# A two-branch mix kernel: first stage on ssm_k in float32 on two row tiles, and the convolution's fill given out in small weighted steps

## The chip, the core and the metric

The kernel runs on one core of a Trainium2 chip. The metric is the device time of one execution in microseconds; the time before the change is the median of three runs, 1002.43 us (1001.9 to 1003.99). The profile comes from one more execution of the same program, which took 1001.61 us.

TensorE (PE in the profile) multiplies matrices into PSUM; VectorE (DVE), ScalarE (ACT) and GpSimd (POOL) work on tiles in SBUF; SyncE (SP), ACT and POOL issue transfers.

## The reference

Two branches on the same 2048 tokens of 512 numbers are mixed by a gate of each token. Branch A is a short causal convolution over 4 taps, a product with `v`, a causal convolution as long as the sequence (computed by FFT) and a product with `q`. Branch B is a mixture of 8 experts, of which each token takes 2.

```python
x = A_q
g = sigmoid((x * gate_w).sum(-1, keepdims=True))

# branch A
k_shift = sum(k_pad[:, t:t+S, :] * shift_k[:, ks-1-t] for t in range(4))
kv = k_shift * v
y = irfft(rfft(pad(kv)) * rfft(pad(ssm_k)))[:S] + kv * ssm_D
a = q * y

# branch B
logits = x @ w_router                    # 8 experts, best 2, softmax over the 2
hg = silu(x @ w_gate[e]);  hu = x @ w_up[e]
b = sum(gate[e] * ((hg * hu) @ w_down[e]) for the 2 experts e)

return g * a + (1 - g) * b
```

## The kernel before

**The main line is the experts.** After routing, the tokens of each expert are gathered in tiles of 128 rows and turned (`gather`, `load_rows`, `turn_rows`, L359 to L395). Each of 8 experts has 11 "up tiles" of up to 128 hidden columns (`FT`), so 88 in all. One up tile (`up`, L752) loads one weight tile `raw`, splits it into a high part (ACT, `gh`) and a rest (DVE, `gl`), and runs, for each of two halves of the expert's tokens and for gate and up, 4 x 3 matmuls: 48 in all. Every product of two float32 matrices is made of three matmuls of float32r parts (`mm3`, L186). After each half ACT takes Silu of the gate's PSUM tile, DVE multiplies by the up's PSUM tile (L784), ACT and DVE split the result (`hh`, `hl`) for the down product. Down products (`down`) and the turning back and scattering of an expert's rows (`finish`, L846) are put into a list `tasks`, of which two are done after each up tile.

**Routing** comes first (L428 to L637) and is written out by hand: inside `tc.manual_schedule` the order of the instructions on every engine is the order of the program (`ordered = True`). It leads from the logits over a ranking on DVE to `list0` (L625), a product that tells which tokens the first expert gets; `read(0)` turns it into indices `gidx` (L597) and POOL gathers the first rows (L366). The rest of the routing (`routing`, L643; `values`, `places` and `read`, L569 to L605) runs beside the first expert's up tiles. Its tiles `hots` and `vals` lie in the second buffers of the tags `xl` and `xh`, so the second expert's rows can only be turned when the last list has been made.

**The convolution is the fill.** It is an FFT in two stages over 16 planes `pl` of 128 rows and 32 frequencies `k1`:

- stage 1 on `ssm_k`, one plane at a time: load `kr`, product with a fixed matrix, two results `t` = 0 and 1 of 128 rows, ACT empties the PSUM tile (L229) and writes it to `kd` in HBM (L230, on ACT's queue)
- stage 1 on `k * v` (`x_stage1`, L271): the four taps on DVE (eight operations of 128x512), a split, the same product, to `xd`
- stage 2 (`x_stage2`, L290): `kd` and `xd` back, products with a matrix of each `k1` (loaded by POOL), the complex product, the way back, to `zd`
- the last stage (`y_stage`, L324): two products that sit side by side on the columns of the array (the second is issued right after the first, L331), times gate and `q`, added to the output.

The product of stage 1 has 64 rows to sum over, for each of `t` = 0 and 1. With `pairs` (L197) the high part of such a half is put on 64 partitions and the rest on the other 64, and two float32r matmuls over 128 partitions do one `t` (L224); with an unsplit tile one float32 matmul over 64 partitions does it (L227), which the trace shows as two records. Six planes (1 to 6) are done inside the hand-written part, at the points `plan(0)` to `plan(4)`, by the string `SEQ` (L57): `o` is a plane's product, `l` a load, `s4` a split of the fifth plane with both subtractions on POOL. The other ten are part of the fill, with one subtraction on POOL and one on DVE (L260).

The fill outside the hand-written part is a list of generators: `k_stage1`, `x_stage1`, `x_stage2`, `y_stage`, with empty entries between (`BUB`). A `tick` (L343) takes one more from the list and moves every live one to its next `yield`. Two ticks are made before the first up tile (L639); then, after each up tile, so many that the count of ticks follows the count of up tiles (L903), to be through at 0.97 of the 88. Outside the hand-written part the program's order is only a priority: a planner with a simulated clock (`schedule_with_timeline_sim`) places the instructions. `after(...)` keeps some of them behind a given instruction of their engine.

PSUM: tag `m` (`misc`) has two buffers for the convolution, tag `y` (`turned`) three, for turned rows, lists and down products, tag `gu` three.

Of the kernel before, what the change touches and what calls it, by code (L numbers as in the profile page):

```python
# [15 lines left out]
ALU = mybir.AluOpType  # L16
# [113 lines left out]
def gated_mix(ctx: ExitStack, tc: tile.TileContext, a, out):  # L130
# [45 lines left out]
    def t2k(tag, bufs, name, dt=F32):  # L176
        return fp.tile([P, D], dt, tag=tag, bufs=bufs, name=name)
# [15 lines left out]
    def rows(t, pl):  # L193
        return t[pl * P:(pl + 1) * P, :]


    def pairs(x, name, eng):  # L197
        ts = []
        for t in range(2):
            own, other = slice(64 * t, 64 * t + 64), slice(64 - 64 * t, 128 - 64 * t)  # L200
            hl = t2k(("fh", "fl")[t], (FH, FL)[t], f"{name}{t}", F32R)
            with after("act k"):
                act.activation(hl[own], x[own], AF.Copy)
            with after("dve k"):
                eng[t].tensor_sub(hl[other], x[own], hl[own].bitcast(F32))
            ts.append(hl)
        return ts

    def load(tag, bufs, name, src, late=False):
# [6 lines left out]
                sync.dma_start(r, src)  # L216
        return r

    def stage1(hl, dst, pl, name):
        for t in range(2):  # L220
            p = misc(f"{name}p{t}")
            if isinstance(hl, list):
                for i in range(2):
                    pe.matmul(p, cr[:, i, :P], hl[t], start=(i == 0), stop=(i == 1))  # L224
            else:
                half = slice(64 * t, 64 * t + 64)
                pe.matmul(p, c1[half], hl[half], start=True, stop=True)  # L227
            ev = t2k("ev", 4, f"{name}e{t}")
            act.activation(ev, p, AF.Copy)  # L229
            act.dma_start(dst[:, :, t::2, pl, :], ev)  # L230

    def mats(src, k1, tag):
        m = fp.tile([P, 2, P], F32R, tag=tag, bufs=3, name=f"{tag}{k1}")
# [1 line left out]
            pool.dma_start(m, src[k1])  # L235
        return m

    kr, ks = {}, {}
# [24 lines left out]

    krows = {}

# [2 lines left out]
            krows[r] = load("A", 6, f"krow{r + 3}", rows(a["kpad"], r + 3))  # L268
        return krows[r]

    def x_stage1(pl):  # L271
        if pl == 0:
            with after("sp"):
                sync.dma_start(sk, a["sk"].unsqueeze(0).to_broadcast([P, TAPS, D]))
        for r in range(-3, 1):
            krow(pl + r)
        v = load("T", 3, f"v{pl}", rows(a["v"], pl))
        yield
        acc = t2k("B", BB, f"acc{pl}")
        tmp = t2k("T", 3, f"tmp{pl}")  # L280
        dve.tensor_mul(acc, krow(pl), sk[:, 0])
        for tap in range(1, TAPS):
            dve.tensor_mul(tmp, krow(pl - tap), sk[:, tap])
            dve.tensor_add(acc, acc, tmp)
        dve.tensor_mul(acc, acc, v)
        hl = pairs(acc, f"xs{pl}", (dve, dve))
        yield
        stage1(hl, xd, pl, f"xs{pl}")

    def x_stage2(k1):  # L290
        flat = lambda t: t[k1].rearrange("c f a d -> (c f a) d")
        rk = load("B", BB, f"kl{k1}", flat(kd))
        rx = load("B", BB, f"xl{k1}", flat(xd))
        mf = mats(a["c_mf"], k1, "mf")
        mi = mats(a["c_mi"], k1, "mi")
        yield
        hk = halves(rk, f"k2{k1}")
        hx = halves(rx, f"x2{k1}")
        yield
        pk = misc(f"k2p{k1}")  # L300
        mm3(pk, mf[:, 0], mf[:, 1], *hk)
        krr = t2k("A", 6, f"krr{k1}")
        kii = t2k("A", 6, f"kii{k1}")
        for t, s0 in ((krr, 0), (kii, 64)):
            for h in range(2):
                act.activation(t[64 * h:64 * h + 64, :], pk[s0:s0 + 64, :], AF.Copy)
        p = misc(f"x2p{k1}")
        mm3(p, mf[:, 0], mf[:, 1], *hx)
        sw = t2k("T", 3, f"sw{k1}")
        act.activation(sw[0:64, :], p[64:128, :], AF.Copy, scale=-1.0)  # L310
        act.activation(sw[64:128, :], p[0:64, :], AF.Copy)
        y = krr
        dve.tensor_mul(y, p, krr)
        dve.tensor_mul(sw, sw, kii)
        dve.tensor_add(y, y, sw)
        hl = halves(y, f"y2{k1}")
        yield
        pz = misc(f"zp{k1}")
        mm3(pz, mi[:, 0], mi[:, 1], *hl)
        ev = t2k("ev", 4, f"ze{k1}")  # L320
        act.activation(ev, pz, AF.Copy)
        act.dma_start(flat(zd), ev)

    def y_stage(pl):  # L324
        r = [load("B", BB, f"zl{pl}_{t}", zd[:, :, t::2, pl, :]) for t in range(2)]
        xr = load("A", 6, f"xr{pl}", rows(a["q"], pl))
        yield

        p = misc(f"yp{pl}")
        last = pe.matmul(p[64:], c2, r[1], start=True, stop=True).ins  # L330
        with tc.issue_after(last):  # L331
            pe.matmul(p[:64], c2, r[0], start=True, stop=True)
        ev = t2k("ev", 4, f"ye{pl}")
        dve.scalar_tensor_tensor(ev, p, G[:, pl:pl + 1], xr, op0=ALU.mult, op1=ALU.mult)
        pool.dma_start(rows(out[:S, :], pl), ev, accum_op=ALU.add)

    wait = lambda n: [iter(()) for _ in range(n)]
    fill = ([k_stage1(i) for i in k_order[SEQ_N:]] + wait(BUB[0]) + [x_stage1(i) for i in range(PL)] + wait(BUB[1]) +
            [x_stage2(i) for i in range(NK)] + wait(BUB[2]) + [y_stage(i) for i in range(PL)])
    fill.reverse()  # L340
    live = []

    def tick():  # L343
        if fill:
            live.append(fill.pop())
        for g in list(live):
            if next(g, live) is live:
                live.remove(g)

    anchor = {}  # L350

# [43 lines left out]
            turn_rows(r, n, g[n], xh, xl)  # L395

    xs = {}

    def ticks(n):
        for _ in range(n):  # L400
            tick()


    CM = max(CAPS)
# [51 lines left out]
    def plan(k):  # L456
        for w in SEQ[k].split():
            i = int(w[1:])
            if w[0] == "l":
                k_load(k_order[i])  # L460
            elif w[0] == "s":
                k_split(k_order[i], (pool, pool))
            else:
                k_out(k_order[i])

# [170 lines left out]
    ordered = False  # L636
    for _ in rows0:  # L637
        pass
    ticks(2)  # L639

    early.close()

# [95 lines left out]
    def expert(r):  # L738
# [13 lines left out]
        def up(ft):  # L752
# [20 lines left out]
            for h, (n0, nn) in enumerate(parts):  # L773
                sl = slice(n0, n0 + nn)
                pp = []
                for u, tag in ((0, "g"), (1, "u")):
                    p = ps.tile([P, 512], F32, tag="gu", bufs=3, name=f"{tag}{r}_{ft}_{h}")
                    for kt in range(KT):
                        mm3(p[:fw, :nn], ghv[:, u, kt], glv[:, u, kt], xh[:, kt, sl], xl[:, kt, sl],
                            start=(kt == 0), stop=(kt == KT - 1))  # L780
                    pp.append(p)
                sg = mp.tile([P, HM], F32, tag="sg", bufs=3, name=f"sg{r}_{ft}_{h}")
                act.activation(sg[:fw, :nn], pp[0][:fw, :nn], AF.Silu)  # L783
                dve.tensor_mul(sg[:fw, :nn], sg[:fw, :nn], pp[1][:fw, :nn])  # L784
# [78 lines left out]

        return begin, up, down, finish

    total, done, seen = len(fill) + len(live), 0, 0
    n_up = E * len(FT) * SPREAD
    tasks = []
    ahead = None
    rest = routing()  # L870
    order_c = [*range(2, len(chunks)), 1]
    for r in range(E):
# [3 lines left out]
        for ft in range(len(FT)):  # L876
# [6 lines left out]
            if r + 1 < E:  # L883
# [15 lines left out]
            seen += 1  # L899
            if r == 0 and ft >= Z0:  # L900
                for i in range(Z1 * (ft - Z0), min(Z1 * (ft - Z0 + 1), ROWS // P)):
                    clear(i)
            while done < min(total, int(total * seen / n_up)):  # L903
                tick()
                done += 1
        if r not in TM:
            tasks += [(finish, n) for n in range(tiles(r))]
    while fill or live:
        tick()
    while tasks:  # L910
        f, *x = tasks.pop(0)
        f(*x)
# [87 lines left out]
```

## Time and profile before

| what | value |
|---|---|
| median of 3 runs | 1002.43 us (1001.9 to 1003.99) |
| profiled execution | 1001.61 us |
| its span, first to last instruction | 999.8 us |
| mean granted TensorE clock | 0.981 |
| PE, weight load, DVE, ACT, POOL busy | 960.8, 881.6, 685.9, 582.5, 182.2 us |
| moved by DMA | 178.19 MB |

A line of a grouped view names the line of the program, the engine, the operation, the tile written and the tiles read, the shape and the count; then the busy time and, after the bar, the idle time of the engine before it and who ended it. A matmul's record is longer than the distance to the next one, since matmuls are pipelined: the distance from start to start is what it costs. A PE that counts as fully busy can still issue more or fewer matmuls.

### The profile page before, as it was taken

What the parts mean: (1) busy time and instruction counts of PE and PEld (TensorE: products, weight loads), DVE (VectorE), ACT (ScalarE), POOL (GpSimd) and SP (SyncE); (2) the same over time, 40 slices, a digit from 0 to 9 for tenths busy, and PEclk for the clock granted to TensorE, in tenths of its full rate; (3) what the DMA queues carried; (4) which work ended last, traced back from release to release, by engine and by line L of the source; (5) the groups of instructions that cost most, each with busy time, mean ns of one, the idle gap of its engine ahead of it and who ended that gap; (6) DMA issues with size and microseconds to landing.
All of it is one profiled execution on the core that took longest, in us unless ns stands there. A gap on an engine that the chain in (4) does not pass through costs nothing. (4 is left out here: it accounts for less than half of the span.)

```text
span 999.8 us, 18820 instructions
## 1 busy us (share of the span) xinstructions
PE 960.8 (96%) x6944; PEld 881.6 (88%) x6944; DVE 685.9 (69%) x1301; ACT 582.5 (58%) x1102; POOL 182.2 (18%) x177
## 2 busy tenths in 40 slices
PE   7888999999999999999999999999999999999995
PEld 2487999989998999999999999998898999768894
DVE  7699679979998855656677468665776666554541
ACT  5485434455555645678667777676777777234230
POOL 1342102110202112131111411022120300113002
PEclk9599999999999999999999999999999999999998
DMA  8775395566656437575445754466565734799613
GB/s 285 249 250 185 112 357 190 167 160 213 201 171 168 147 115 215 176 166 169 137 142 180 181 180 159 141 187 141 156 195 159 206 117 135 217 327 241 162 31 42
DMA packets 88401, 178.19 MB, mean 178 GB/s; under 512 B 10641, under 2 KB 19601, under 8 KB 88178
## 3 DMA queue, kind: packets, MB, share of 16 engines
q1 hardware_dynamic: 52882, 116.73, 35.6%
q0 software_dynamic: 19296, 30.08, 15.3%
q10 hardware_dynamic: 16128, 30.15, 8.3%
q8 instruction: 56, 0.92, 0.4%
q14 instruction: 39, 0.32, 0.1%
HBM read 133.34 MB, written 43.57 MB: 177 GB/s over the span
## 5 line engine op out<-in xcount | busy, mean ns | idle before, releaser
L187 PE MATMUL g<-xh,gh 128*128 128x256 f32 (+13 forms) x704 | 203.9, 290 | 5.6 <-DVE sg L784 5.6
L187 PE MATMUL u<-xh,gh 128*128 128x256 f32 (+13 forms) x704 | 202.0, 287 | 6.0 <-ACT sg L783 5.1
L189 PE MATMUL g<-xh,gl 128*128 128x256 f32 (+13 forms) x704 | 201.6, 286 | 0.0
L188 PE MATMUL g<-xl,gh 128*128 128x256 f32 (+13 forms) x704 | 201.5, 286 | 0.0
L188 PE MATMUL u<-xl,gh 128*128 128x256 f32 (+13 forms) x704 | 201.2, 286 | 0.0
L189 PE MATMUL u<-xh,gl 128*128 128x256 f32 (+13 forms) x704 | 201.1, 286 | 0.0
L187 PEld LDWEIGHTS g<-xh,gh 128*128 128x128 f32 (+1 forms) x704 | 131.5, 187 | 15.7 <-DVE sg L784 8.8
L187 PEld LDWEIGHTS u<-xh,gh 128*128 128x128 f32 (+1 forms) x704 | 131.2, 186 | 10.8 <-ACT sg L783 6.9
L784 DVE TENSOR_TENSOR sg<-sg,u 128x256 f32<-128x256 f32 (+13 forms) x176 | 74.9, 426 | 90.5 <-PE u L189 56.4
L188 PEld LDWEIGHTS g<-xl,gh 128*128 128x128 f32 (+1 forms) x704 | 131.6, 187 | 3.1
L189 PEld LDWEIGHTS u<-xh,gl 128*128 128x128 f32 (+1 forms) x704 | 131.3, 186 | 3.1 <-issue 1.6
L188 PEld LDWEIGHTS u<-xl,gh 128*128 128x128 f32 (+1 forms) x704 | 131.2, 186 | 2.7 <-issue 0.8
L189 PEld LDWEIGHTS g<-xh,gl 128*128 128x128 f32 (+1 forms) x704 | 131.7, 187 | 1.3
L187 PE MATMUL yp<-hh,dh 128*128 128x266 f32 (+10 forms) x440 | 128.0, 292 | 2.1 <-ACT yr L853 1.9
L188 PE MATMUL yp<-hl,dh 128*128 128x266 f32 (+10 forms) x440 | 127.4, 290 | 0.0
L189 PE MATMUL yp<-hh,dl 128*128 128x266 f32 (+10 forms) x440 | 127.1, 290 | 0.0
L768 DVE TENSOR_TENSOR gl<-raw,gh 128x1024 fp32r<-128x1024 f32 (+1 forms) x88 | 105.2, 1195 | 28.4 <-ACT gh L766 26.3
L783 ACT ACTIVATE sg<-g 128x256 f32<-128x256 f32 (+13 forms) x176 | 67.5, 385 | 87.0 <-PE g L189 83.0
L766 ACT ACTIVATE gh<-raw 128x1024 fp32r<-128x1024 f32 (+1 forms) x88 | 91.3, 1037 | 40.9 <-PE u L188 30.1
L785 ACT ACTIVATE hh<-sg 128x256 fp32r<-128x256 f32 (+13 forms) x176 | 73.6, 419 | 70.1 <-DVE sg L784 68.9
L786 DVE TENSOR_TENSOR hl<-sg,hh 128x256 fp32r<-128x256 f32 (+13 forms) x176 | 75.2, 428 | 36.8 <-ACT hh L785 35.9
L366 POOL DMA_INDIRECT xg<-in_q,gidx x37 | 48.5, 1311 | 227.0 <-PE xgp L375 209.4
(1072 smaller groups left out, 1898.3 us busy)
## 6 DMA issues: line engine op xcount, KB each, us to landing
raw<-in_wgu SPq DMA_DIRECT2D x77, 512.0 KB
rd<-in_wd SPq DMA_DIRECT2D x77, 256.0 KB
kl<-kd SPq DMA_DIRECT2D x32, 256.0 KB
xl<-xd SPq DMA_DIRECT2D x32, 256.0 KB
zd<-ze ACTq DMA_DIRECT2D x32, 256.0 KB
zl<-zd SPq DMA_DIRECT2D x32, 256.0 KB
out<-zt SPq DMA_DIRECT2D x21, 256.0 KB
krow<-in_kpad SPq DMA_DIRECT2D x19, 256.0 KB
```

The source lines that it names most:

```text
L187: pe.matmul(p, wh, hi, start=start, stop=False)
L188: pe.matmul(p, wh, lo, start=False, stop=False)
L189: pe.matmul(p, wl, hi, start=False, stop=stop)
L366: anchor["pool"] = pool.indirect_dma_start(out=xg[:w], out_offset=None, in_=a["q"], in_offset=bass.IndirectOffsetOnAxis(ap=gidx[:w, col:co ...
L766: act.activation(gh[:, :n], raw[:, :n], AF.Copy)
L768: dve.tensor_sub(gl[:, :n], raw[:, :n], gh[:, :n].bitcast(F32))
L783: act.activation(sg[:fw, :nn], pp[0][:fw, :nn], AF.Silu)
L784: dve.tensor_mul(sg[:fw, :nn], sg[:fw, :nn], pp[1][:fw, :nn])
L785: act.activation(hh[:fw, sl], sg[:fw, :nn], AF.Copy)
L786: dve.tensor_sub(hl[:fw, sl], sg[:fw, :nn], hh[:fw, sl].bitcast(F32))
```

## The change

Stage 1 on `ssm_k` no longer splits. Every plane is done in float32 by two matmuls over 64 partitions each, on the upper and the lower half of the array's rows; both PSUM tiles are taken first, `t` = 1 is issued before `t` = 0, and outside the hand-written part `t` = 0 is held right behind it. In the hand-written part even planes take their PSUM tiles from tag `y`. `s4` and its branch are gone, as are `k_split` and the two early ticks.

The generators become lists of steps, each with a place (relative to its item's number), a weight and a function. `woven` sorts the steps of all items of a stage by place, and adds a pause. The steps are given out by weight, as far as the share of up tiles done allows, at four points of each up tile: after each half, at its end, and after the tasks. The taps of `x_stage1`, one step before, are in three steps, its split in a fourth; stage 2 has five steps.

```diff
-BUB = (1, 1, 3)
-SEQ = "|o0 l5 o1|o2 s4 o3||o4 o5".split("|")
+SEQ = "|o0 l5 o1|o2 o3||o4 o5".split("|")
...
+    def out1(p, dst, pl, t, name):
+        ev = t2k("ev", 4, f"{name}e{t}")
+        act.activation(ev, p, AF.Copy)
+        act.dma_start(dst[:, :, t::2, pl, :], ev)
+
     def stage1(hl, dst, pl, name):
         for t in range(2):
             p = misc(f"{name}p{t}")
-            if isinstance(hl, list):
-                for i in range(2):
-                    pe.matmul(p, cr[:, i, :P], hl[t], start=(i == 0), stop=(i == 1))
-            else:
-                half = slice(64 * t, 64 * t + 64)
-                pe.matmul(p, c1[half], hl[half], start=True, stop=True)
-            ev = t2k("ev", 4, f"{name}e{t}")
-            act.activation(ev, p, AF.Copy)
-            act.dma_start(dst[:, :, t::2, pl, :], ev)
+            for i in range(2):
+                pe.matmul(p, cr[:, i, :P], hl[t], start=(i == 0), stop=(i == 1))
+            out1(p, dst, pl, t, name)
+
+    def stage1_f32(x, dst, pl, name):
+        where = turned if ordered and pl % 2 == 0 else misc
+        ps_ = [where(f"{name}p{t}") for t in range(2)]
+        first = None
+        for t in (1, 0):
+            half = slice(64 * t, 64 * t + 64)
+            with tc.issue_after(first) if first is not None and not ordered else nullcontext():
+                first = pe.matmul(ps_[t], c1[half], x[half], start=True, stop=True).ins
+        for t in range(2):
+            out1(ps_[t], dst, pl, t, name)
...
-    def k_split(pl, engines):
-        ks[pl] = pairs(kr[pl], f"ks{pl}", engines)
-
     def k_out(pl):
-        stage1(ks.get(pl, kr[pl]), kd, pl, f"ks{pl}")
-
-    def k_stage1(pl):
-        if pl not in kr:
-            k_load(pl)
-            yield
-        if pl not in ks:
-            k_split(pl, (pool, dve))
-            yield
-        k_out(pl)
+        stage1_f32(kr[pl], kd, pl, f"ks{pl}")
+
+    def k_steps(pl):
+        yield -1.5, .3, lambda: k_load(pl)
+        yield 0, 1.3, lambda: k_out(pl)
...
+    def x1_steps(pl):
...
+        yield -1.2, .3, fetch
+        yield 0, 2.1, lambda: taps(0, 2)
+        yield .25, 1.4, lambda: taps(2, 3)
+        yield .5, 2.1, lambda: taps(3, 4)
+        yield .75, 1.4, split
+        yield 1.3, 1.0, lambda: stage1(t["hl"], xd, pl, f"xs{pl}")
...
+    def x2_steps(k1):
...
+        yield -1.9, .3, fetch
+        yield -.8, 1.4, split
+        yield 0, 1.0, forward_k
+        yield .3, 3.5, forward_x
+        yield 1.2, 1.0, back
...
+    def y_steps(pl):
...
+        yield -1.2, 2.0, fetch
+        yield 0, 2.5, turn
...
+    def woven(items, pause):
+        steps = [(i + at, i, w, do) for i, item in enumerate(items) for at, w, do in item]
+        steps.sort(key=lambda x: x[:2])
+        return [(w, do) for _, _, w, do in steps] + [(pause, lambda: None)]
+
+    fill = (woven([k_steps(i) for i in k_order[SEQ_N:]], 3) + woven([x1_steps(i) for i in range(PL)], 6) +
+            woven([x2_steps(i) for i in range(NK)], 9) + woven([y_steps(i) for i in range(PL)], 0))
+    load_all = sum(w for w, _ in fill)
+    spent = [0.0]
+
+    def fill_to(share):
+        while fill and spent[0] + fill[0][0] / 2 <= share * load_all:
+            w, do = fill.pop(0)
+            spent[0] += w
+            do()
...
-    ticks(2)
...
             for h, (n0, nn) in enumerate(parts):
...
                 dve.tensor_sub(hl[:fw, sl], sg[:fw, :nn], hh[:fw, sl].bitcast(F32))
+                fill_up(.25 + .25 * h)
...
             st[ft] = (hh, hl, dh, dl)
+            fill_up(.75)
...
+    def fill_up(part):
+        fill_to((seen[0] + part) / n_up)
...
-            while done < min(total, int(total * seen / n_up)):
-                tick()
-                done += 1
+            fill_up(0)
...
-    while fill or live:
-        tick()
+    fill_to(2)
```

More of the change, by code (lines that the diff above doesn't have):

```diff
@@ L236, in mats @@
         return m
-    kr, ks = {}, {}
+    kr = {}
     k_order = [*range(1, PL), 0]
@@ L269, in krow @@
         return krows[r]
[L271 to L288, printed above, removed]
@@ L290, in x_stage2 @@
-    def x_stage2(k1):
-        flat = lambda t: t[k1].rearrange("c f a d -> (c f a) d")
[L292 to L348, printed above, removed]
+    def x1_steps(pl):
+        t = {}
+        def fetch():
+            if pl == 0:
+                with after("sp"):
+                    sync.dma_start(sk, a["sk"].unsqueeze(0).to_broadcast([P, TAPS, D]))
+            for r in range(-3, 1):
+                krow(pl + r)
+            t["v"] = load("T", 3, f"v{pl}", rows(a["v"], pl))
+        def taps(first, last):
+            if first == 0:
+                t["acc"] = t2k("B", BB, f"acc{pl}")
+                t["tmp"] = t2k("T", 3, f"tmp{pl}")
+                dve.tensor_mul(t["acc"], krow(pl), sk[:, 0])
+            for tap in range(max(first, 1), last):
+                dve.tensor_mul(t["tmp"], krow(pl - tap), sk[:, tap])
+                dve.tensor_add(t["acc"], t["acc"], t["tmp"])
+            if last == TAPS:
+                dve.tensor_mul(t["acc"], t["acc"], t["v"])
+        def split():
+            t["hl"] = pairs(t["acc"], f"xs{pl}", (dve, dve))
+        yield -1.2, .3, fetch
[4 more added lines that the diff above has]
+        yield 1.3, 1.0, lambda: stage1(t["hl"], xd, pl, f"xs{pl}")
@@ new lines, in y_steps, with fetch, turn @@
+    def y_steps(pl):
+        t = {}
+        def fetch():
+            t["r"] = [load("B", BB, f"zl{pl}_{h}", zd[:, :, h::2, pl, :]) for h in range(2)]
+            t["xr"] = load("A", 6, f"xr{pl}", rows(a["q"], pl))
+        def turn():
+            p = misc(f"yp{pl}")
+            last = pe.matmul(p[64:], c2, t["r"][1], start=True, stop=True).ins
+            with tc.issue_after(last):
+                pe.matmul(p[:64], c2, t["r"][0], start=True, stop=True)
+            ev = t2k("ev", 4, f"ye{pl}")
+            dve.scalar_tensor_tensor(ev, p, G[:, pl:pl + 1], t["xr"], op0=ALU.mult, op1=ALU.mult)
+            pool.dma_start(rows(out[:S, :], pl), ev, accum_op=ALU.add)
+        yield -1.2, 2.0, fetch
+        yield 0, 2.5, turn
@@ L397, in gated_mix @@
     xs = {}
-    def ticks(n):
-        for _ in range(n):
-            tick()
     CM = max(CAPS)
@@ L460, in plan @@
                 k_load(k_order[i])
-            elif w[0] == "s":
-                k_split(k_order[i], (pool, pool))
             else:
@@ L864, in expert @@
         return begin, up, down, finish
-    total, done, seen = len(fill) + len(live), 0, 0
+    seen = [0]
     n_up = E * len(FT) * SPREAD
+    def fill_up(part):
+        fill_to((seen[0] + part) / n_up)
     tasks = []
@@ L898, in gated_mix @@
                     next(ahead, None)
-            seen += 1
+            seen[0] += 1
             if r == 0 and ft >= Z0:
```

36 lines of the change are left out of this document (35 added, 1 removed).

## The prediction

> **What bounds the kernel now.** I read the page first, then the busy times by stage, then who ended PE's waits, then the timeline of the stages where PE is not full.
>
> ```profile
> span 999.8 us, 18820 instructions
> PE 960.8 (96%) x6944; PEld 881.6 (88%) x6944; DVE 685.9 (69%) x1301; ACT 582.5 (58%) x1102; POOL 182.2 (18%) x177
> ```
> ```profile
> 20.00:44.00 24.00, 19.36 (x57) 7.79 (x56) 15.79 (x54) 10.85 (x19) 8.00 (x7) 0.55 0.68 231
> 57.00:95.00 38.00, 32.04 (x219) 29.20 (x217) 37.43 (x76) 24.38 (x46) 10.16 (x7) 1.00 0.66 219
> 95.00:120.00 25.00, 24.20 (x219) 23.17 (x220) 19.44 (x48) 10.56 (x21) 5.97 (x4) 1.00 0.33 109
> 150.00:220.00 70.00, 67.78 (x519) 66.98 (x519) 61.92 (x113) 34.17 (x67) 14.52 (x10) 1.00 0.60 184
> 220.00:300.00 80.00, 80.00 (x602) 78.29 (x601) 77.49 (x140) 43.32 (x83) 9.07 (x5) 1.00 0.56 184
> 300.00:340.00 40.00, 36.28 (x266) 35.11 (x265) 32.43 (x57) 22.11 (x44) 8.91 (x5) 0.96 0.60 165
> 340.00:860.00 520.00, 517.19 (x3792) 492.26 (x3791) 335.86 (x607) 363.79 (x690) 89.47 (x102) 1.00 0.56 163
> ```
>
> The columns of the second view are the stretch, its length, then PE, PEld, DVE, ACT and POOL, granted clock, DMA share, GB/s. PE bounds the kernel: from 340 to 860 us it lacks 2.8 us of 520. So relief of other engines is worth nothing there. What can be gained is PE's missing time elsewhere: 38.00 - 32.04 = 6.0 us in 57 to 95, 0.8 in 95 to 120, 2.2 + 3.7 = 5.9 in 150 to 220 and 300 to 340, and the start, where PE waits for routing. The row of 220 to 300 matters too: DVE at 77.49 of 80 and PE full, so a DVE filled with taps does not by itself stop PE.
>
> ```profile
> PE g L187 <- DVE sg L784: 4.1, 3, 1.4
> PE u L187 <- DVE sg L784: 0.8, 1, 0.8
> ```
> ```profile
> PE u L187 <- ACT sg L783: 4.0, 2, 2.2
> PE yp L187 <- ACT yr L853: 1.9, 1, 1.9
> ```
> ```profile
> ACT yr L853 <- DMA out<-yr,sidx: 25.7, 10, 5.9
> ```
>
> The first two rows are PE's waits in 55 to 95, the next two those in 200 to 350, the last is of the whole run (total, times, longest). Early, PE waits for DVE, which is late with the product that frees a gate or up PSUM tile. Later it waits behind ACT, whose queue stands at L853 until an older scatter has let go of `yr`.
>
> **Why DVE is late early.**
>
> ```profile
> L205 POOL TENSOR_TENSOR ks<-kr,ks x12: 1261/1456/1832, 30.3 to 97.2; 64x512 fp32r<-64x512 f32 x12
> L205 DVE TENSOR_TENSOR ks<-kr,ks x10: 686/687/1665, 57.0 to 100.8; 64x512 fp32r<-64x512 f32 x10
> ```
> ```profile
> 47.72 0.21 DVE L652 TENSOR_TENSOR s<-s 128x64 f32<-128x64 f32 x1
> 47.85 0.22 DVE L654 TENSOR_SCALAR r<-r 128x128 f32<-128x128 f32 x1
> ```
> ```profile
> 54.45 1.31 DVE L656 TENSOR_TENSOR s<-s,rc 128x64 f32<-128x64 f32 x1
> ```
>
> The split of `ssm_k` costs DVE ten subtractions of 0.69 us, and more through POOL: beside a subtraction on POOL an operation that takes DVE 0.21 us (L652) takes 1.31 (L656, same shape). With some eight such collisions after 50 us, at 1.1 us each, the split holds DVE for about 10 x 0.69 + 8 x 1.1 = 16 us of the 44 us to 101, an estimate from these rows.
>
> **The change part by part.**
>
> *The start.* The fifth plane's split on POOL sits on routing's path:
>
> ```profile
> 27.55 3.67 PE L227 MATMUL ks4p<-kr,c 64*128 64x512 f32 x4
> 28.02 2.35 DVE L614 TENSOR_TENSOR hots<-u,rc 128x1024 bf16<-128x1024 f32 x2
> 30.26 2.61 POOL L205 TENSOR_TENSOR ks<-kr,ks 64x512 fp32r<-64x512 f32 x2 [11.34 <-ACT ks L203]
> 30.48 1.12 DVE L619 TENSOR_SCALAR r<-r 128x128 f32<-128x128 f32 x1
> 31.15 0.59 PE L628 MATMUL list<-vals,hots 128*128 128x10 bf16 x16
> 31.64 1.38 DVE L620 TENSOR_TENSOR r<-r,r 128x128 f32<-128x128 f32 x1
> 33.47 0.22 DVE L594 TENSOR_SCALAR idf<-list,late 128x5 f32<-128x5 f32 x1
> 34.98 1.63 POOL L366 DMA_INDIRECT xg<-in_q,gidx  x1 [2.11 <-DVE gidx L597]
> 39.30 1.11 PE L375 MATMUL xgp<-ident,xg 128*128 128x128 f32 x4 [1.83 <-DMA xg<-in_q,gidx]
> ```
>
> L619 and L620 lie between `hots` and the reading of the list (L594). They take 1.12 and 1.38 us beside POOL; L619's like, L654, takes 0.22, and I take 0.3 for L620. So L594 can start 0.9 + 1.1 = 2.0 us earlier, if the list is there: it ends at 31.74, behind plane 4's 3.67 us on PE, and without that from 30.37, when `hots` is done, about 0.7 us earlier. Plane 4 does get shorter: 3.67 us because the second product waited for the first one's PSUM tile, while plane 1 shows what two free tiles give:
>
> ```profile
> 19.75 1.13 PE L227 MATMUL ks1p<-kr,c 64*128 64x512 f32 x4
> ```
>
> The gathers and the first turned rows (39.30) follow `gidx`. What eats some of it is the clock, 0.55 in this stretch: if it rises no earlier than now, the 2 us of work brought forward run at half speed and 1.0 us is left. I take -1.5, bounds -2.6 (the list's 0.6 also counting) and -1.0. The Trainium skill, "TensorE: Matmul & The Clock Gate", section "Part 1: The HAM clock gate (the "warmup" mystery)", has the clock return after a busy window of about 3.4 us whose phase does not depend on the kernel; by that rule the saving is either end and not the middle, which this trace cannot decide.
>
> *57 to 95.* With the split gone from POOL and DVE, the 4.9 us of waits for `sg` should largely go. The fast fill brings something back: by the weights of the diff a plane on `ssm_k` is 1.6, all ten with the pause 19, a plane of the taps 8.3, that stage 138.8, stage 2 239.4, the last 72, together 469.2 over 0.97 x 88 = 85.4 up tiles, 5.5 to one. So the taps start at up tile 3.5 (about 75 us) instead of 150, run 25 up tiles instead of some 18, stage 2 takes 44 and the last stage 13. I take -4.5, bounds -6.0 (all of PE's missing time) and 0 (taps fill every gap).
>
> *The product itself.* Ten planes in the fill go from four float32r matmuls to two float32 ones. The latter's pair is not in the fill's trace; the nearest row is the last stage's pair, side by side on columns:
>
> ```profile
> 863.61 0.27 PE L189 MATMUL g<-xh,gl 128*96 128x252 f32 x1
> 863.82 0.64 PE L330 MATMUL yp<-zl,c 128*64 128x512 f32 x1
> 863.82 0.64 PE L332 MATMUL yp<-zl,c 128*64 128x512 f32 x1
> 864.83 0.49 PE L187 MATMUL yp<-dh,hh 128*120 128x512 f32 x1
> ```
> ```profile
> 83.81 0.28 PE L189 MATMUL u<-xh,gl 128*128 128x256 f32 x1
> 83.92 1.09 PE L224 MATMUL ks10p<-ks,cr 128*128 128x512 f32 x4
> 84.85 0.31 PE L187 MATMUL g<-xh,gh 128*128 128x312 f32 x1
> ```
>
> From the matmul ahead to the one behind: 864.83 - 863.61 = 1.22 us for the pair, 84.85 - 83.81 = 1.04 for the four. So a plane costs 0.18 us more, ten 1.8 us, on a full PE. Upper bound: the two tiles run one after the other (the other's PSUM tile is late, or something slips between), then the pair's 1.01 us comes twice, +10 us more, +12. Lower bound 0. I take +1.8: L330 and L332 start together, and so do plane 1's two in the row above (four records in 1.13 us where ks4 took 3.67). The rule that speaks against it is in the Trainium skill, "TensorEngine Tiling (Array Packing)", "Key Properties": a change of tiling mode drains TensorE. It gives no price; the 0.21 us ahead of L330 may hold it, which the sum has. The ACT evictions and writes to `kd` are as many as before; each plane loses two splits on ACT.
>
> *The taps' stage.* Same work, earlier and thinner. Each plane moves eight DVE operations and two subtractions:
>
> ```profile
> L283 DVE TENSOR_TENSOR tmp<-krow,sk x48: 678/684/694, 149.8 to 341.4; 128x512 f32<-128x512 f32 x48
> L205 DVE TENSOR_TENSOR xs<-acc,xs x32: 684/686/689, 164.8 to 348.6; 64x512 fp32r<-64x512 f32 x32
> ```
>
> That is 10 x 0.685 = 6.9 us a plane, and two loads on SP's queue (behind the up tiles' weights), two writes on ACT's, two evictions. One plane per 1.5 up tiles instead of 1.1 takes DVE from 77.49 of 80 to about 75% (estimate). The 5.9 us of waits behind ACT at 205 and 318 to 326 come in this stage; five later experts in 340 to 860 cost 2.8 in all. So a looser DVE may free scatters sooner. I take -2.0, bounds -5.9 and +2 (a stall at another place).
>
> *Taps beside routing.* Between 75 and 150 us about 7 up tiles give out 7 / 1.5 = 4.6 planes, 32 us of DVE; the rows show 0.6 + 5.6 us of DVE free in 57 to 120, the gone split frees perhaps 8 after 75, and 120 to 150 has some 7 (at 95 to 120's 22%). That is 21: some 11 us are pushed past 150. What is queued behind a tap is routing's lists and the experts' L784. I take +0.5, bounds 0 and +8.
>
> *Stage 2, the last stage, the tail*: as many operations; PE is full either way. 0, bounds -3 and +3.
>
> Sum: -1.5 - 4.5 + 1.8 - 2.0 + 0.5 = -5.7 us. The profiled execution takes 1001.61 (span 999.8 and 1.8 around it), so 995.9; the median of the runs is 0.8 above that execution, so **996.7 us**.
>
> **The rivals.**
>
> *A larger gain.* All waits in 57 to 95 (-6.0) and the start's -2.6 go, both finishes (-5.9), the pair costs 1.8, stage 2 gives 2: -14.7, 988. For it: all of these are waits, not work. Against: the finishes wait for a scatter that the change does not touch.
>
> *Slower: the taps hold up the second expert's rows.*
>
> ```profile
> 148.53 0.64 PE L375 MATMUL xgp<-ident,xg 128*128 128x128 f32 x4
> ```
> ```profile
> 170.77 0.28 PE L187 MATMUL g<-xh,gh 128*128 128x278 f32 x1
> ```
>
> The second expert's first rows are turned at 148.53 and its first up matmul runs at 170.77. Three turned tiles take some 8 us, so about 14 us are spare. If planner and queue place taps ahead of the lists, all of the 32 us less the 8 that the split gives back, and less the 6 free up to 120, delay them: 18 us, 4 over; with the slow return of the clock after such a gap and two gathers in series on POOL, say 8, plus PE's waits in 57 to 95 staying: -1.5 + 1.8 - 2.0 + 8 = +6, 1009. It decides from a delay of 14 us on. The Trainium skill, "SBUF — State Buffer", section "🔬 SBUF: two separate sides", says that a VectorE operation with two SBUF inputs and a GpSimd one lock each other out for whole instructions; L656's 1.31 us agrees, and by that rule taps also slow POOL's gathers, whose first here takes 1.63 us. Against the rival: lists stand earlier in the program.
>
> *Slower too: the row tiles run one after the other.* -5.7 + 10 = +4.3, 1006.7. For it: ks4 in the hand-written part. Against: that was one PSUM tile too few.
>
> *It doesn't do what it says*: the waits in 57 to 95 stay, now behind taps. -5.7 + 4.5 = -1.2, 1001.2, which can't be told from no change (0.2%, 2 us, is the limit).
>
> **How the numbers follow.** The forecast has 0.50, the larger gain 0.18, the second expert's rows 0.13, the serial tiles 0.07, waits that stay 0.12. The forecast's own range is 990 to 1000. The first two, with a tenth of the last, make faster by over 0.2% 0.69; no change 0.09; slower 0.22, the slower rivals and the last one's upper side. The range 984 to 1008 leaves out a little of the larger gain below, and above the second expert's case in half.
>
> **What would show it.** Right: no `ks` rows of L205; L619 and L620 near 0.25 us; first turned rows near 37.5; PE's missing time in 57 to 95 near 1.5; pairs that start together, 1.2 us from matmul to matmul. Wrong: pairs with starts 1 us apart; a first turned row of the second expert after 162 us and a gap in PE behind it; PE missing time in 340 to 860 well over 2.8, which would mean that steps given out at four points disturb the up tiles themselves, a cost that I have at nothing because ACT and DVE have time there (363.79 and 335.86 of 520).

## The result, and the profile after

The changed kernel takes 1004.98 us (median of 22 runs, 1002.02 to 1009.7) where the kernel before takes 1002.3 beside it (22 runs): a ratio of 1.003, 95% interval 1.0019 to 1.0041. It is 2.7 us slower by the medians and 3.0 by the ratio, and the forecast was 996.7. The profiled execution takes 1006.17 us, its span is 1004.4.

First the stages, in the same columns as before the change (stretch and length, then PE, PEld, DVE, ACT, POOL busy with the count of instructions, granted clock, DMA share, GB/s). The first row is of the kernel before, the others of the changed one:

```profile
44.00:57.00 13.00, 12.53 (x80) 11.74 (x80) 9.75 (x22) 10.69 (x17) 4.86 (x3) 0.79 0.94 301
```
```profile
44.00:57.00 13.00, 8.68 (x43) 7.25 (x42) 4.41 (x13) 6.00 (x12) 0.00 (x0) 0.63 0.95 347
57.00:95.00 38.00, 38.00 (x230) 27.25 (x228) 33.60 (x91) 17.75 (x35) 3.04 (x1) 1.00 0.78 263
150.00:220.00 70.00, 68.43 (x540) 66.77 (x539) 61.96 (x117) 31.83 (x60) 14.48 (x8) 1.00 0.56 174
220.00:300.00 80.00, 78.08 (x592) 76.87 (x593) 74.33 (x130) 43.06 (x84) 7.69 (x6) 1.00 0.48 148
300.00:340.00 40.00, 38.69 (x299) 37.58 (x298) 22.97 (x44) 19.67 (x39) 10.12 (x8) 1.00 0.60 157
340.00:860.00 520.00, 518.75 (x3810) 492.01 (x3809) 337.15 (x600) 367.23 (x693) 90.75 (x103) 1.00 0.58 168
```

The stretch 57 to 95 is full now (38.00 of 38, before 32.04). Yet the first up tile ends 5.7 us later than before, at 59.67, the fourth 11.2 us later, at 91.97 (last matmul starts of each). Some 1 to 2 us of this is scatter of one execution: plane 1's product already starts at 21.64 here, at 19.75 before, and at 19.71 to 20.84 in the runs further down. So PE is busier and has got less far: 230 matmuls in 38.00 us of work against 219 in 32.04, and of these only 170 belong to up tiles, against 197. And 44 to 57 is worse, 8.68 against 12.53. After up tile 15 the changed kernel is 18.0 us behind, but it has more of its fill done there (28 matmuls of the taps' stage against 8). At up tile 77, where both have done the same, it is 6.1 us behind (880.72 against 874.60), and 4.3 at the last. Two things explain the first 100 us.

**The products of a plane stand apart.** The timeline of PE in the changed kernel, one plane of the fill (start, length, then line, tile and shape; an `x2` is the two records of one float32 product):

```profile
64.57 1.12 PE L238 MATMUL ks8p<-kr,c 64*128 64x512 f32 x2
65.62 0.41 PE L187 MATMUL g<-xl,gh 128*128 128x312 f32 x1
65.87 0.30 PE L188 MATMUL g<-xh,gl 128*128 128x312 f32 x1
66.11 1.12 PE L238 MATMUL ks8p<-kr,c 64*128 64x512 f32 x2
67.16 0.41 PE L186 MATMUL g<-xh,gh 128*128 128x312 f32 x1
```

From the first product's start to the next matmul is 65.62 - 64.57 = 1.05 us, from the second's again 67.16 - 66.11 = 1.05. A product alone, on 64 of the 128 rows, costs as much as both together where they are neighbours (1.06 us, further down). Of the ten planes of the fill eight stand apart like this; only ks7 and ks11 have their two products next to each other. `issue_after` puts `t` = 0 behind `t` = 1, and keeps nothing else from between.

**The taps' first loads stand ahead of the first rows.** SP's own queue, then PE, then ACT in the changed kernel:

```profile
29.37 0.35 SPq L798 DMA_DIRECT2D raw<-in_wgu  x1
29.76 0.43 SPq L280 DMA_DIRECT2D sk<-in_sk  x1
30.24 1.08 SPq L215 DMA_DIRECT2D v<-in_v  x2
33.16 6.34 SPq L215 DMA_DIRECT2D krow<-in_kpad  x4
```
```profile
34.02 1.05 POOL L408 DMA_INDIRECT xg<-in_q,gidx  x1 [13.20 <-DVE gidx L633]
```
```profile
41.32 1.09 PE L417 MATMUL xgp<-ident,xg 128*128 128x128 f32 x4 [5.60 <-DMA xg<-in_q,gidx]
48.82 0.58 PE L186 MATMUL g<-xh,gh 128*128 128x256 f32 x1 [3.56 <-ACT xh L419]
```
```profile
41.07 0.33 ACTq L221 DMA_DIRECT2D kd<-ks5e  x1
41.44 0.60 ACT L220 ACTIVATE ks5e<-ks5p 128x512 f32<-128x512 f32 x1 [5.63 <-DMA v<-in_v]
47.79 0.34 ACTq L796 DMA_DIRECT2D raw<-in_wgu  x1
48.17 0.60 ACT L419 ACTIVATE xh<-xgp 128x512 fp32r<-128x512 f32 x1 [3.08 <-DMA rd<-in_wd]
```

The view of DMA issues gives `sk` 1 MB and each `v` and `krow` 256 KB. In the kernel before, SP issues nothing between the first weights (27.73) and 54.55. Here the taps' loads follow the first weights at once. The gather is issued at 34.02 and its rows are turned 7.30 us later (4.32 before, from 34.98 to 39.30). ACT, which issues writes and loads in its own order, stands 5.63 us before an eviction and 3.08 us before the `xh` that the first up matmul needs. That matmul comes at 48.82 instead of 43.80.

What holds ACT can be read from the semaphores in the trace. In this program the DMAs that SP and ACT issue report their landing to eight semaphores in turn, and an issue waits until the DMA before it on the same semaphore has landed. The write of `ks5e` is issued at 41.07: it shares its semaphore with the second `v` load, which SP issued at 30.74 and which landed at 40.99. ACT's weight loads at 45.37, 46.26 and 47.79 follow the landings of three `krow` loads (45.34, 46.24, 47.77). Everything behind such an issue on ACT waits with it. So a load on SP's queue can hold ACT without using ACT's queue.

### The profile page after: what moved, and what is told of

Same layout as the page of the kernel before. It is cut to its first block, busy times and chain, and to the rows that moved or that the text cites. A ratio compares the mean times of both kernels' runs of the same rounds, so it can differ in the third digit from the quotient of the medians.

```text
span 1004.4 us, 18688 instructions
## 1 busy us (share of the span) xinstructions
PE 964.9 (96%) x6944; PEld 876.9 (87%) x6944; DVE 673.0 (67%) x1291; ACT 571.8 (57%) x1080; POOL 166.3 (17%) x165
```

## The experiments

Medians are in us, and each ratio is to the kernel before, measured beside it on the same chip (median 1001.84 to 1002.73), so 0.001 is 1 us. Differences between two runs are differences of these ratios. From both 95% intervals they are uncertain by 2 to 3.3 us, and the medians can put them up to 2 us elsewhere.

**The pairs side by side, first try.** One PSUM tile of two banks for the whole program, whose halves tag `m` gives out in turn:

```diff
+    m2 = ps.tile([P, 2, D], F32, tag="m", bufs=1, name="m2")
...
     def misc(name):
-        return ps.tile([P, D], F32, tag="m", bufs=2, name=name)
+        m_n[0] += 1
+        return m2[:, (m_n[0] + 1) % 2]
```

> The changed kernel with one edit: the two PSUM buffers of the convolution are two halves of one tile, used in turn, so that the product of t = 1 waits for the later of the two evictions and t = 0 can follow at once. Theory A (in the changed kernel 8 of 10 planes of the fill have their two row tiles one after the other, with up matmuls between, at 1.15 us a plane): ten pairs that start together, some 9 us less than the changed kernel's 1005, so 994 to 998. Theory B (the whole loss is made before the first up tile, by the taps' early loads; serial tiles are hidden): within 2 us of 1005.

Measured 1007.77, ratio 1.0047 (1.0028 to 1.0065): a miss. But all ten planes stand together, and at up tile 77 the kernel is 8.5 us ahead of the kernel before (866.07 against 874.60). It loses 10 us between there and the end of the up tiles (976.05 against 974.23 at the last), in the last stage, which has the fixed halves as well. Not all of that lead was progress: by up tile 77 it had run none of the last stage's products, where the kernel before had run four planes of them, at 1.01 us each.

**The taps' loads later, by moving a weight load.** `QN` is (1, 2) instead of (1, 2, 3), so that the fourth up tile's weights go on SP's queue and the taps' loads are held behind them.

> The changed kernel with one constant changed: the fourth up tile's weights are loaded on SP's queue (QN = (1, 2)), so that the taps' first nine loads, which stand behind the last weights traced on SP, are issued after about 50 us instead of 30 us. Theory B (these loads hold up the first gathers and the writes to kd, whose buffers ACT waits for, 5.7 us): first up matmul near 43 instead of 48.8 us, 999 to 1001. Theory A alone (serial row tiles are all of it): 1004 to 1006. If both hold, 999 to 1001 too, and the next kernel tells them apart.

Measured 1005.6, ratio 1.0036 (1.0018 to 1.0054): as the change, which is what theory A alone allowed. The first up matmul came at 42.72, as theory B expected, but up tile 2 ended at 71.23, later than the 69.70 of the change. **Both edits together:**

> Both edits in one. If A and B each hold and add up: 1005 - 9 - 5 = 991, 988 to 994. If only A holds, 996; if only B holds, 1000. If neither, 1005.

Measured 1010.75, ratio 1.0064 (1.004 to 1.0089), outside all four expectations and above either, though the intervals overlap. Both edits had a second effect, so nothing could be added up from these three.

**The new product alone**, in the kernel before, with its generators and ticks as they were:

> The kernel before with the float32 product on two row tiles alone, the fill given out in ticks as before. No tap is loaded early here. My sum for this part: start -2, no split on POOL and DVE -4.5, pairs +1.8, so 1002.3 - 4.7 = 997.6; where four planes have their tiles apart, as the order of the instructions has it, +4.6 more: 1002. Theory that the loss of the changed kernel lies in the fill's new steps and not in the product: 996 to 1000. Theory that the product itself costs it: 1004 or more.

Measured 997.13, ratio 0.9934 (0.9914 to 0.9954). This part of the change gains 6.6 us, within the range for a loss that lies in the fill's new steps. Its row for 57 to 95, and two rows of its start:

```profile
57.00:95.00 38.00, 38.00 (x306) 33.39 (x306) 35.15 (x87) 16.95 (x35) 5.42 (x4) 1.00 0.67 223
```
```profile
31.06 0.29 DVE L623 TENSOR_TENSOR r<-r,r 128x128 f32<-128x128 f32 x1
36.48 0.63 PE L380 MATMUL xgp<-ident,xg 128*128 128x128 f32 x4 [1.09 <-DMA xg<-in_q,gidx]
```

306 matmuls in the same 38.00 us, where the whole change has 230. They are not alike: 183 belong to up tiles, 45 to down products, 64 are the short list products and 14 records of planes; in the change 170, none, 32 and 28. At the old pace (a plane at a tick) only two of ten planes stand apart.

**The fill in small steps alone**, with the old split product (weights .2, .6, .8 for load, split and product):

> The kernel before with the fill in small steps at four points alone; the product on ssm_k stays the split one on four float32r matmuls (weights .2 for the load, .6 for the split, .8 for the product). Theory (the new fill brings its loads forward past the first gathered rows and packs ten splits into three up tiles): 1006 to 1012 us, first up matmul near 48 us. Rival (the loss of the change is only in the serial float32 products, which are not here): 1000 to 1003 us.

Measured 1012.52, ratio 1.0095 (1.0075 to 1.0115). It is half a microsecond above the expected range. The fill costs time with no float32 pair in it. Its first turned rows come at 43.36, its first up matmul at 46.79 (expected near 48), and the waits for DVE that the product removes are back and longer (7.4 us here against 4.1 in the kernel before, from 55 to 95):

```profile
43.36 1.11 PE L409 MATMUL xgp<-ident,xg 128*128 128x128 f32 x4 [4.07 <-DMA xg<-in_q,gidx]
```
```profile
PE g L186 <- DVE sg L813: 7.4, 4, 2.2
```

Its second expert's first rows are turned at 171.8, past the 162 that the prediction named as a sign, and PE stands 2.07 us behind them, at 175.0. How the 9.5 us divide among early loads, splits and this stays open.

**The pairs side by side, kept to the planes.** The double tile lives only until the fill's last plane on `ssm_k`; then its banks go to two single tiles:

```diff
+    pk = ExitStack()
+    both = pk.enter_context(tc.tile_pool(name="both", bufs=1, space=PSUM)).tile([P, 2, D], F32, tag="m2", name="both")
+    single, turn_ = [], [0]
     def misc(name):
-        return ps.tile([P, D], F32, tag="m", bufs=2, name=name)
+        if single:
+            return single[0].tile([P, D], F32, tag="m", bufs=2, name=name)
+        turn_[0] += 1
+        return both[:, turn_[0] % 2]
+    def planes_done():
+        pk.close()
+        single.append(ctx.enter_context(tc.tile_pool(name="single", bufs=2, space=PSUM)))
...
-    fill = (woven([k_steps(i) for i in k_order[SEQ_N:]], 3) + ...
+    fill = (woven([k_steps(i) for i in k_order[SEQ_N:]], 3) + [(0, planes_done)] + ...
```

> The changed kernel with the two PSUM tiles of a plane's product on ssm_k cut from one double tile until the fill's planes are done, and two single tiles after that, so that the two products of a plane stand next to each other on PE while the last stage has its tiles back. Theory (row tiles that run apart cost the changed kernel about 9 us, and the first pairs experiment lost it again only in the last stage, through its fixed halves): the lead of 8 us over the kernel before at the 77th up tile stays to the end, 995 to 998 us, and no wait of PE at 922 to 936 us. Rival (the end is set by something else, and a lead is given back there): 1003 to 1007 us, with the gaps at 922 to 936 us again.

Measured 999.47, ratio 0.9958 (0.994 to 0.9976): 7.2 us less than the change, though above the 995 to 998 expected. No wait stands at 922 to 936 us any more. The lead of 8 us at up tile 77 is not there: with the same fill done, that tile ends at 874.54, level with the kernel before, and the last one 1.9 us ahead of it (972.34 against 974.23).

```profile
63.79 1.13 PE L249 MATMUL both<-kr,c 64*128 64x512 f32 x4
64.85 0.41 PE L199 MATMUL g<-xh,gl 128*128 128x312 f32 x1
```
```profile
57.00:95.00 38.00, 38.00 (x297) 30.73 (x296) 36.41 (x98) 19.38 (x38) 4.24 (x2) 1.00 0.81 267
```

Both products take 64.85 - 63.79 = 1.06 us. 297 matmuls fit where the change has 230. Of the 67 more, 31 belong to up tiles and down products (0.12 to 0.14 us each from start to start), 32 are list products (0.59 / 16 = 0.04 us each in the kernel before), and 4 are the records of one plane. That is some 6 us, near the 7.2 at the end. Five planes that stand apart in this stretch of the change cost 5 x 1.05 = 5.3 us. The Trainium skill, "TensorEngine Tiling (Array Packing)", section "Key Properties", says that different tiles can load weights and multiply in parallel. The 1.06 us for two beside 1.05 for one agrees, and the change shows what it takes: the two have to be neighbours in the queue.

**The taps a little later**, pause 8 instead of 3, without and with the double tile:

```diff
-    fill = (woven([k_steps(i) for i in k_order[SEQ_N:]], 3) + ...
+    fill = (woven([k_steps(i) for i in k_order[SEQ_N:]], 8) + ...
```

> The changed kernel with the pause after the planes of ssm_k at 8 instead of 3, which traces the first loads of the taps about one up tile later, behind the weights of an up tile on SP's queue; no weights load is moved. Theory (loads of the taps that stand ahead of the first gathered rows cost some 5 us up to the first up matmul, and the late_fetch run gave these back only because it moved the fourth up tile's weights): first turned rows near 36.5 us, first up matmul near 42.7, and of this 4 us are left at the end, 1000 to 1002 us. Rival (the early loads cost nothing that lasts, the time is set by the serial products and by what comes later): 1004 to 1006 us.

> Both edits of e5_pairs_kept and e6_late_taps. Theory (the two losses add up, and nothing else of the change costs time): 990 to 994 us, below the kernel with only the new product (997.1). Rival (the fill's steps at four points cost something of their own): 997 us or more.

Measured 1016.82, ratio 1.0127 (1.0098 to 1.0157), and 1010.17, ratio 1.0073 (1.0055 to 1.0092): both theories missed, the delay made it worse. The first is outside its rival's range too and scatters widely (1011.76 to 1021.23, the profiled execution the slowest); the second lies in its rival's range, but its trace points to the loads, not to the four points. In the second of them the first up tile is in time (53.75), and then the loads land on the next weights, on the planes' loads and on the writes to `kd`:

```profile
57.00:95.00 38.00, 32.78 (x256) 27.20 (x255) 34.56 (x79) 15.51 (x32) 5.58 (x4) 0.96 0.95 335
```
```profile
56.48 1.07 ACT L231 ACTIVATE ks8e<-both 128x512 f32<-128x512 f32 x2
59.01 0.38 ACTq L223 DMA_DIRECT2D kr<-in_ssk  x1
63.37 2.27 ACTq L232 DMA_DIRECT2D kd<-ks8e  x2
65.68 0.38 ACT L829 ACTIVATE sg<-g 128x256 f32<-128x256 f32 x1 [8.13 <-DMA kr<-in_ssk]
```
```profile
66.12 0.63 PE L197 MATMUL u<-xh,gh 128*128 128x312 f32 x1 [5.22 <-ACT sg L829]
```

The DMA engines are 0.95 busy. The write of `ks8e`, ready at 57.55, is issued at 63.37, after the load of `sk` on its semaphore has landed at 63.30; its second half follows a `krow` load that landed at 65.23. The Silu behind them runs after 8.13 us of idle time on ACT, and PE stands 5.22 us for it. In the run without the double tile, PE also waits 7.9 us in 340 to 860, 4.0 of it for an eviction of stage 2; the reason stays open.

**The taps as late as before the change**, pause 40, without and with the double tile:

> The changed kernel with the pause after the planes of ssm_k at 40 instead of 3: the taps start about when they start in the kernel before (up tile 9 to 10), the products stay as in the change, most of them apart. Theory (taps' loads in the first six up tiles hold up weights and the in-order queue of ACT, whose writes to kd wait behind them; that is also why pause 8, which moved the loads onto the second up tile's weights, was worse): up1 near 53.7 us, no wait of PE for sg above 2 us in 57 to 95, and only the serial products' 5 to 9 us left against the kernel with the new product alone: 1001 to 1006 us. Rival (the later the taps, the worse, because their work then has fewer up tiles): 1015 us or more.

> Pause 40 and the double PSUM tile of e5_pairs_kept. Theory (serial products and early taps are the two losses, and the steps at four points are free): 994 to 998 us. Rival (the steps at four points, or ten planes within three up tiles, cost something of their own): 1000 us or more.

Measured 1001.74, ratio 0.9993 (0.9977 to 1.001), and 995.56, ratio 0.9926 (0.9898 to 0.9954), both as the theory said. Eight planes stand apart in the first, none in the second: 6.7 us between them, beside the 7.2 above. The late taps are worth 3.2 us with the double tile (from 0.9958, uncertain by 3.3) and 3.7 without (from 1.003, uncertain by 2.0).

```profile
36.30 1.09 PE L428 MATMUL xgp<-ident,xg 128*128 128x128 f32 x4 [0.82 <-DMA xg<-in_q,gidx]
```

**Loads or work?** The same kernel as the last, with `sk`, five rows of `kpad` and two of `v` alone brought forward to where the change loads them:

```diff
-    fill = (woven([k_steps(i) for i in k_order[SEQ_N:]], 40) + [(0, planes_done)] + ...
+    fill = (woven([k_steps(i) for i in k_order[SEQ_N:]], 3) + [(0, planes_done), (.3, early_loads), (36.7, lambda: None)] + ...
```

> e10_pairs_pause40, and only the first loads of the taps (sk, five rows of kpad, two of v) are brought forward to where the changed kernel issues them, behind the first weights on SP's queue; the taps' work stays where pause 40 puts it. Theory (the loads alone take the early loss, by standing before the gathered rows and the first weights): first turned rows near 40, first up matmul near 47.5 us instead of 41.4, and 998 to 1001 us at the end. Rival (the loss is the taps' work on DVE and ACT beside routing): the first up matmul is late as well, but the end stays at 995 to 997 us.

Measured 1000.14, ratio 0.9984 (0.997 to 0.9998), 5.8 us above the kernel without them (4.6 by the medians, uncertain by 3.1).

```profile
38.92 1.08 PE L436 MATMUL xgp<-ident,xg 128*128 128x128 f32 x4 [5.13 <-DMA xg<-in_q,gidx]
46.24 0.58 PE L197 MATMUL g<-xh,gh 128*128 128x256 f32 x1 [3.40 <-ACT xh L438]
```
```profile
43.64 0.34 ACTq L846 DMA_DIRECT2D rd<-in_wd  x1
45.20 0.34 ACTq L815 DMA_DIRECT2D raw<-in_wgu  x1
45.59 0.60 ACT L438 ACTIVATE xh<-xgp 128x512 fp32r<-128x512 f32 x1 [4.71 <-DMA krow<-in_kpad]
```

The gather's issue is as early as without (32.08 and 32.24), its rows are turned 2.6 us later, and the first up matmul stands 4.9 us later (46.24 against 41.37). The rest of the delay is ACT's: it stands 4.71 us ahead of an `xh` of the first rows, behind two weight issues that follow the landings of `krow` loads (43.62 and 45.18). So eight loads of 2.75 MB in all, seven of them issued from 27.83 to 35.80, carry the early loss as far as these runs can tell; the taps' work on DVE at the early place (the double tile with pause 3, 0.9958) shows no cost beyond that.

**Slow planes**, weights 1.2 and 5.2 instead of .3 and 1.3:

> The changed kernel with the weights of a plane on ssm_k at 1.2 and 5.2 instead of .3 and 1.3, nothing else: ten planes over some eleven up tiles as in the kernel before, and the taps after them. Theory (the pace set by the weights is the loss: planes that come faster than ACT gives the PSUM tiles back stand apart, and the taps come too early): like the kernel with the new product alone, 996 to 1000 us. Rival (steps at four points cost something of their own): 1002 us or more.

Measured 1002.19, ratio 0.9999 (0.9979 to 1.002): the theory missed, and the number lies in the rival's range. Five planes still stand apart, three more than with the new product alone. That is some 2.5 us at the 0.84 a plane of pause 40 (6.7 / 8); of the 6.5 us against the new product alone the remaining 4 stay open. The rival's own cause, the four points, is not borne out by the next run.

**Fewer points**, pause 40 and the double tile, with the fill given out only at the end of an up tile:

```diff
-                fill_up(.25 + .25 * h)
...
-            fill_up(.75)
```

> e10_pairs_pause40 with the fill given out only at the end of each up tile, the same weights and shares. Theory (the four points cost nothing and give little): within 2 us of 995.6. Rival (the four points are worth something, as steps then fall on PE, DVE and ACT in lumps): 998 us or more; the other rival (they disturb the up tiles): 993 us or less.

Measured 993.64, ratio 0.9919 (0.9903 to 0.9935). It is the fastest of all, but its interval and that of four points (0.9898 to 0.9954) overlap: the four points give nothing that these runs show. What they cost is 0.7 us by the ratios and 1.9 by the medians, which is within the noise. One of its ten planes stands apart.

## Why the prediction was wrong

The waits were read rightly, and the two terms for what the change adds were not.

**The start, -1.5: right as far as the first up matmul shows.** In the change L656 (L620 before) takes 0.29 us instead of 1.38:

```profile
32.38 0.29 DVE L656 TENSOR_TENSOR r<-r,r 128x128 f32<-128x128 f32 x1
```

With the new product alone the list starts at 29.62 instead of 31.15, 1.5 us earlier, the first rows are turned at 36.48, 2.8 earlier, and the first up matmul comes at 42.46, 1.3 earlier. In the change the early loads hide that.

**57 to 95, -4.5: right in mechanism.** The waits for `sg` there are gone, but PE's missing time was the wrong measure of progress once planes and lists filled it. The view of waits for 55 to 95 has one row left:

```profile
PE g L187 <- DVE xl L420: 0.7, 1, 0.7
```

**The product, +1.8: the step that failed.** "I take +1.8: L330 and L332 start together, and so do plane 1's two" took the price of a pair from places where the program keeps the two as neighbours. The pair's price there holds (1.06 us); that the fill's pairs would be such pairs does not. In the fill 8 of 10 planes stand apart, and the double tile gives back 6.7 to 7.2 us. The rival that names it, "the row tiles run one after the other", had 0.07, with "that was one PSUM tile too few" against it. That its 1006.7 lies close to 1004.98 is partly luck: its sum has no cost of early loads and a smaller gain of the new product than was measured. The trace of before could not show this. The diff could: the wait in it only orders the two, and outside the hand-written part the planner decides what goes between. For all eight planes apart both PSUM tiles had been free for 1.4 us or more when PE ran them. For ks8 the writes behind the evictions of ks7 had been issued by 62.43, ahead of the first product at 64.57.

```profile
62.43 0.33 ACTq L221 DMA_DIRECT2D kd<-ks7e  x1
```

So it was the order laid down ahead of the run that held them apart, not a wait on the chip. That the planner counted the second tile as free later than the first is likely, and no run shows it by itself.

**The taps' stage, -2.0, and taps beside routing, +0.5: the second step that failed.** "Two loads on SP's queue (behind the up tiles' weights)" is where the loads were costed, at nothing. They were behind the first weights alone, because weights 1 to 3 are issued by ACT and the hold is on SP's last. The prediction had the taps start at about 75 us; their first operation on DVE came at 89.91, but their first load at 29.76, since the planner could bring it forward to there. The early loads cost 3.2 to 5.8 us: they delay the first rows, and they hold ACT's issues through the shared semaphores. The term looked at DVE, where 32 us of taps were to find room, and no run shows a cost of that. PE's missing time in 150 to 340 did fall, from 5.9 to 4.8 us (1.57 + 1.92 + 1.31), 1.1 instead of 2.0. The second expert's first rows, turned at 160.1 instead of 148.5, came within the 162 allowed, and PE has no gap behind them before 217 us.

**The four points at nothing: holds.** In 340 to 860 PE lacks 1.25 us of 520, and the run without three of the points is not clearly faster.

So the two steps that failed can be added to what the new product alone gave: -6.6 with two planes apart, six more apart at 0.84 are +5.0, and the early loads are +3.2 to +5.8. That makes +1.6 to +4.2, and +3.0 was measured. The steps for the start, 57 to 95 and the product gave -4.2 together where the new product alone gave -6.6; where the larger gain comes from stays open.

## What to carry to other kernels

Two matmuls on halves of the array are worth one only as neighbours in PE's queue. If a planner places the work, give them one tile that comes free as a whole, and count in the trace how many pairs are neighbours. When a stage is moved forward, cost its loads first: name the queue, what holds them back there, and which transfer on the critical path is in flight at that time. Look at semaphores that DMAs of several engines share, since a load of one engine can then hold the issue of another. A delay that only moves the collision to the next transfer can be worse than none. A full PE is no proof of progress: compare the count of like matmuls in the stretch, or when the same up tile ends with the same fill done.

## What the runs showed of the hardware

A float32 product over 64 partitions and 512 columns takes 1.05 us from start to the next matmul, alone or with its twin on the other half. In this program ACT's issue of a DMA waits for an older DMA on the same semaphore, one of SP's too: a write ready at 57.55 was issued at 63.37, after a load of SP's had landed at 63.30, and everything behind it on ACT waited. With four of the early loads ahead of the first gather on SP's queue and three behind it, the gather's rows, asked for by POOL, were turned 6.84 us after its issue (38.92 - 32.08) instead of 4.06 (36.30 - 32.24).
